# Block-wise causal attention and a gated feed-forward layer: four of six pairs of hidden chunks as seven block products in tiles 3 to 6, all six in tiles 7 and 8, all issued from written lists

## The chip, the cores and the metric

The kernel runs on one NeuronCore of a Trainium2 chip. The metric is the device time of one execution in microseconds (us), the median of the runs shown. A core has five engines with an instruction queue each, and each queue is worked off in order: PE (TensorE, the matrix engine; its weight loads are listed as PEld), DVE (VectorE), ACT (ScalarE), POOL (GpSimd) and SP (SyncE, here only a queue for transfers). Engines wait for each other by semaphores. The matrix engine writes to PSUM, eight banks of 128 x 512 float32; everything else is in SBUF, 128 partitions wide.

## The reference

```python
scores = scale * np.matmul(q, k.transpose(0, 1, 3, 2))      # q, k, v: 8 x 8 x 576 x 64
mask = block_i >= block_j                                   # blocks of 64 rows
attn = np.exp(...) / (np.sum(...) + 1e-09)
x = (attn @ v).transpose(0, 2, 1, 3).reshape(4608, 512)
gate = np.maximum(x @ w_gate, 0.0)                          # 512 x 1536
val = x @ w_val
return (gate * val @ w_out).astype(np.float32)              # 1536 x 512
```

## The kernel before, in words

**Tiles.** The 576 rows of a batch are cut into 512 and a tail of 64. Tile j (0 to 7) is the feed-forward layer of the 512 rows of batch j, tile 8 that of the eight tails together, 512 rows again. `x` lies transposed in `xT` (tile 8: `xTt`), four row groups of d_model by 512 tokens. The 1536 hidden columns are twelve chunks of 128. The work of tile j is interleaved on PE with the attention of batch j+1, which needs no more than that: per batch four rounds (one pair of heads each) of scores (`visit`, L465), exponentials on ACT (L470 and L477), products with v (L600, L614), their normalisation on DVE (L537 to L546) and a transpose by a transfer on SP's queue (L647). Loads of batch j+2 are 17 transfers issued by POOL (`load_qkv`, L353).

**A plain chunk.** Gate and value of chunk f are four matmuls each (`product`, L948; 128 x 512 elements out), ACT makes the ReLU into SBUF (`relu`, L958), DVE multiplies it with the value bank into `hT` (`hidden`, L968; L995 in tiles 7 and 8).

**Seven block products.** A product of two matrices cut 2 x 2 takes eight products of blocks, or, by Strassen's scheme, seven products of sums of blocks (numbered 1 to 7 in the code) and additions. The kernel uses this at two places. The projection to the output in tiles 2 to 8 (`seven_products`, L830) takes 84 matmuls of 256 columns per tile, numbered M below; DVE makes the sums of `hT` for it (`Sums`, L789), POOL and DVE made those of `wo` once (L706 to L720). And in tiles 7 and 8 the gate and value of a pair of chunks (`by_pairs`, `pair` and `times`, L1014; `PAIRS = (2, 4, 6)`: chunks 2 and 3, 4 and 5, 6 and 7) take 28 matmuls of 256 columns in place of 16 of 512. Here one matrix has the halves of d_model as rows and gate and value as columns, the other the halves of d_model and of the tokens. A pair uses three banks, `y`, `z` and `m1`. ACT copies y and z out, POOL adds these two copies (L1045), DVE subtracts them from m1 (L1048), adds the result to y and to z after further products were accumulated there (L1055, L1057), and two products give `hT` (L1058, on DVE or POOL; L1062). The sums of token halves, `x_sums`, are five DVE instructions per tile (L940), those of weights, `up_sum`, fifteen in tiles 5 and 6 (L747).

**What sets the order.** Each engine's queue is in the order in which the program emits. A generator `ffn_gen` emits the feed-forward work matmul by matmul; a table `AT` (and `STEADY` for later batches) says after how many of these each piece of attention, load or weight sum is emitted. Buffers are rotating: `psum_ffn` has three banks (`ffnp`), `psum_sc` two pairs of banks (`sc`), `psum_one` one (`one`), `ob` five SBUF buffers, `gate_sb` three, `stage` ten, `hT` three. An instruction that takes a buffer waits until the last reader of the buffer's former content has ended.

Of the kernel before, what the change touches and what calls it, by code (L numbers as in the profile page):

```python
# [17 lines left out]
def kernel(  # L18
# [22 lines left out]
    PAIRS = (2, 4, 6)  # L41
    BASE = {0: 0, 1: 512, 3: 896, 2: 1024}
    AW = 1600
    TW = 256

# [78 lines left out]
    class Early:  # L124
# [152 lines left out]
        def pe_mains(self, hp, evac, two=None, ts=(0, 1)):  # L277
            if two is None:
                two = {t: psum_ffn.tile([128, 512], BF, name="ffnp") for t in ts}
# [20 lines left out]
        def pe_tails(self, evac):  # L300

            tq = psum_ffn.tile([128, 4, 64], BF, name="ffnp")
            tk = psum_ffn.tile([128, 4, 128], BF, name="ffnp")
# [13 lines left out]
    def load_qkv(b, which, behind=None):  # L317
        for t in which:
            src = (q, k, v)[t]
            for c in range(NCH):  # L320
# [31 lines left out]
                for dst, part_of in pieces:  # L352
                    ins = nc.gpsimd.dma_start(dst, part_of)  # L353
                    after(ins, behind)
                    behind = None

    bfs = {}

    def dma_transposes(b):
        m, tl = bfs[b, 0], bfs[b, 1]  # L360
        for t in range(2):
# [4 lines left out]
        tails_by_dma(b, tl)  # L366
# [32 lines left out]
    def bank(where, dtype=FP):  # L399

        n = 512 if dtype == FP else 1024
        if where == "sc":
            return psum_sc.tile([128, 2, n], dtype, name="sc")[:, 0, :]
        if where == "one":
            return psum_one.tile([128, n], dtype, name="one")
        return psum_ffn.tile([128, n], dtype, name="ffnp")

    def scores(b, hp, pieces):
        sc = psum_sc.tile([128, 2, 512], FP, name="sc")
# [26 lines left out]
    def thirds():  # L436
        return (
            psum_one.tile([128, 512], FP, name="one"),
            psum_ffn.tile([128, 512], FP, name="ffnp"),
        )  # L440

    def visit(r):
# [3 lines left out]
        first = psum_sc.tile([128, 2, 512], FP, name="sc")  # L446
        second = psum_sc.tile([128, 2, 512], FP, name="sc")
# [26 lines left out]
        def exp_third():  # L474
            for hh in range(2):
# [4 lines left out]

        return exp_third, exp(first, 0), exp(second, 512)

    def last_keys(b):
# [10 lines left out]
        nc.scalar.activation(attnL[b % 2][:, 0:256], last, AF.Exp, scale=scale)  # L494

    def tail_visit(b):

        main = [psum_sc.tile([128, 2, 512], FP, name="sc") for _ in range(2)]
# [34 lines left out]
    def normalise(out, av, x=None):  # L533
        n = av.shape[1]
        rows = av.shape[0]
        recip = sb.tile([128, NCH], FP, name="recip", bufs=4)[0:rows, 0:n]
# [16 lines left out]
    def tail_av(b, g, x):  # L553

        av = psum_ffn.tile([128, 4, 65], FP, name="ffnp")
# [16 lines left out]
        recip = sb.tile([128, NCH], FP, name="recip", bufs=4)  # L572
# [18 lines left out]
    def products_with_v(r, hh, av):  # L591
# [17 lines left out]
        if b >= FIRST:  # L609
# [3 lines left out]
            for c in range(NCH):  # L613
# [9 lines left out]
                )  # L623
        normalise(xnats[r][:, :, 64 * hh : 64 * hh + 64], av, x)

    def head_av(r, hh, where):
        n = 5 if r // 4 >= FIRST else 4
        av = bank(where)[:, 0 : 65 * n].rearrange("q (p e) -> q p e", e=65)
        products_with_v(r, hh, av)
# [25 lines left out]
    store, late = [], []  # L655
# [65 lines left out]

    ups = {}

    def up_sum(n, which):
# [4 lines left out]
        if not ups:  # L729
            ups["free"] = [  # L730
                t[:, 512 * i : 512 * i + 512].rearrange("p (c f) -> p c f", c=2)
                for two in (new_bf(), new_bf())
                for t in two
                for i in range(4)
            ]
# [10 lines left out]
        t = ups[n, which] = ups["free"].pop(0)  # L746
        nc.vector.tensor_tensor(out=t, in0=a, in1=b, op=op)  # L747

    class Sums:
# [3 lines left out]
        def __init__(self, quads):  # L753
            self.quads = quads
            self.two = []
# [52 lines left out]
    def seven_products(j, quads, sums):  # L808
# [33 lines left out]
        early, last = ((0, 1, 2, 3), (4, 5)) if j < B - 1 else ((0, 1, 2, 4), (3, 5))  # L842

        def whole(to, which, new=True, cs=range(6)):
            for p in range(2):
                for c in cs:
                    times(half(to, p), which, p, c, new and (p, c) == (0, 0))
                    if c % 2:
                        yield

        def store_later(hi, n0, ob, p0=0, p1=2):
            if store:
                store.pop()()
            if j < B:
                store.append(lambda: put_block(j, hi, n0, ob, p0, p1))
            else:
                put_block(j, hi, n0, ob, p0, p1)

        y = psum_ffn.tile([128, 512], FP, name="ffnp")
        z = psum_one.tile([128, 512], FP, name="one")  # L860
        for to, which in ((y, 5), (z, 2)):
            yield from whole(to, which, cs=early)
        for to, which in ((y, 5), (z, 2)):
            yield from whole(to, which, new=False, cs=last)
        for q in range(3) if j >= B - 1 else ():
            sums.make_part(q, 1, 0, 2)
        g = sb.tile([128, 512], FP, name="ob", bufs=5)
        nc.scalar.copy(g, y)
        nc.vector.tensor_tensor(out=g, in0=z, in1=g, op=AX.add)
        for q in range(3) if j >= B - 1 else ():  # L870
            sums.make_part(q, 2, 0, 2)
        m1 = psum_ffn.tile([128, 512], FP, name="ffnp")
        yield from whole(m1, 1)
        nc.vector.tensor_tensor(out=g, in0=m1, in1=g, op=AX.subtract)
        if j == B - 1:
            x_sums(B, (1, 3))
        yield from whole(y, 3, new=False)
        c12 = sb.tile([128, 512], FP, name="ob", bufs=5)
        nc.scalar.copy(c12, y)  # L879
        store_later(0, 256, c12)  # L880
        c22 = sb.tile([128, 512], FP, name="ob", bufs=5)
        nc.gpsimd.tensor_tensor(out=c22, in0=g, in1=c12, op=AX.add)  # L882
        yield from whole(z, 4, new=False)
        c21 = sb.tile([128, 512], FP, name="ob", bufs=5)
# [930 lines left out]
```

## Time and profile before

| | |
|---|---|
| median of 3 runs | 351.77 us (351.35 to 353.55) |
| span of the profiled execution, first to last instruction | 350.5 us |
| what lies around the span, against the median | 1.27 us |
| tiles 0 and 1 with all that precedes them | 0 to 104.0 us |
| tile 2 | 104.0 to 141.08 us |
| tiles 3, 4 and 5, each | 37.15 us |
| tile 6 | 252.52 to 288.47 us, 35.95 us |
| tile 7 | 288.47 to 317.18 us, 28.71 us |
| tile 8 and the last stores | 317.18 to 350.5 us; last matmul about 345.7 us |
| granted TensorE clock | 0.999 of full |

The page gives no time of this execution but its span; the difference to the median is what is carried along for start and end. The tiles' borders are where a tile's plain matmuls (L948) begin in the chain that ended last. A matmul that the trace lists with 379 ns is not 379 ns of the engine: consecutive matmuls overlap, and what one costs is the distance from one start to the next.

### The profile page before, as it was taken

Reading aid. Unit: us, or ns where it says so; the run is one execution under the profiler, and the core shown is the slowest. Engines: PE = TensorE matmul, PEld = TensorE weight load, DVE = VectorE, ACT = ScalarE, POOL = GpSimd, SP = SyncE. Lnnn points to the kernel's source line nnn. Section 1 sums busy time; section 2 is a strip of 40 time slices with the busy share of each in tenths; the row PEclk is TensorE's granted clock in tenths of the full one; section 3 lists DMA queues with packets and bytes.
Section 4 is the critical chain, followed back from the end, with each engine's and each line's share of the span. In section 5 each row is a group of like instructions: output and inputs, shape, how many; then the busy total and the mean of one; then the engine's idle time right before and its main releaser. Section 6 shows DMA issues by size and latency. Waiting matters only on the chain.

```text
span 350.5 us, 8275 instructions
## 1 busy us (share of the span) xinstructions
PE 339.8 (97%) x3210; PEld 208.2 (59%) x3254; DVE 225.5 (64%) x564; ACT 185.2 (53%) x297; POOL 153.8 (44%) x194
## 2 busy tenths in 40 slices
PE   8999999999999999999999999999999999999994
PEld 3544455545445568545855576556755687687673
DVE  4853455667529784467547772668567867986892
ACT  5933766687235862666355545555366525423521
POOL 2767556576598902590149203950300022213213
PEclk9999999999999999999999999999999999999999
DMA  8999989999999994999459974999510031003005
GB/s 240 295 353 373 352 224 248 222 148 155 184 185 153 144 182 98 138 147 169 62 134 141 104 135 123 127 131 150 121 47 17 16 94 50 2 2 121 1 2 120
DMA packets 155399, 50.02 MB, mean 143 GB/s; under 512 B 134464, under 2 KB 151744, under 8 KB 155360
## 3 DMA queue, kind: packets, MB, share of 16 engines
q0 software_dynamic: 70528, 8.98, 49.1%
q1 hardware_dynamic: 77520, 32.52, 44.0%
q10 hardware_dynamic: 7312, 8.00, 7.8%
q8 instruction: 25, 0.41, 0.5%
q14 instruction: 14, 0.11, 0.1%
HBM read 37.75 MB, written 9.44 MB: 135 GB/s over the span
## 4 chain that ended last, share of the span: by engine, by line
PE 77%; DMA 14%; POOL 3%; issue 2%; DVE 2%; ACT 1%; SPq 1%; POOLq 0%; ACTq 0%
PE ffnp L948 39%; PE ffnp L830 12%; PE one L830 5%; PE sc L1014 3%; DMA stage<-in_moe_w_out_dram 3%; PE sc L465 3%; DMA xT<-xnat 2%; DMA stage<-in_moe_w_val_dram 2%; PE one L465 2%; DMA stage<-in_v_dram 2%; DMA stage<-in_moe_w_gate_dram 2%; PE ffnp L600 2%; PE one L600 2%; PE ffnp L1181 2%; PE one L1014 2%
## 5 line engine op out<-in xcount | busy, mean ns | idle before, releaser
L958 ACT ACTIVATE gate_sb<-ffnp 128x512 bf16<-128x512 f32 x95 | 57.1, 605 | 74.8 <-PE ffnp L948 66.5
L948 PE MATMUL ffnp<-xT,wg 128*128 128x512 bf16 x338 | 93.0, 379 | 1.7 <-issue 0.6
L948 PE MATMUL ffnp<-xT,wv 128*128 128x512 bf16 x309 | 87.7, 380 | 1.0 <-DVE hT L968 0.3
L968 DVE TENSOR_TENSOR hT<-gate_sb,ffnp 128x512 bf16<-128x512 bf16 x76 | 51.9, 683 | 46.0 <-PE ffnp L948 27.0
L948 PEld LDWEIGHTS <-wv 128*128 128x128 bf16 x384 | 35.4, 98 | 38.2 <-issue 4.6
L470 ACT ACTIVATE attnT<-sc 128x1024 bf16<-128x1024 f32 x56 | 57.0, 1042 | 0.0
L948 PEld LDWEIGHTS <-wg 128*128 128x128 bf16 x384 | 35.7, 98 | 35.0 <-issue 1.7
L882 POOL TENSOR_TENSOR ob<-ob 128x512 f32<-128x512 f32 x7 | 9.6, 1370 | 101.7 <-ACT ob L879 53.3
L830 PEld LDWEIGHTS <-stage 128*128 128x128 bf16 x420 | 40.3, 98 | 6.0
L789 DVE TENSOR_TENSOR stage<-hT 128x512 bf16<-128x512 bf16 (+2 forms) x82 | 37.8, 493 | 0.9
L600 PEld LDWEIGHTS <-attnT 128*128 128x128 bf16 x640 | 26.7, 98 | 11.9 <-DVE attnT L1241 0.9
L830 PE MATMUL ffnp<-stage 128*128 128x256 bf16 x252 | 31.4, 273 | 0.0
L353 POOL DMA_DIRECT2D v_bf<-in_v_dram x30 | 24.1, 869 | 6.1 <-DVE recip L537 2.6
L477 ACT ACTIVATE attnT<-one 128x512 bf16<-128x512 f32 (+1 forms) x28 | 15.0, 536 | 21.1 <-PE ffnp L465 21.1
L353 POOL DMA_DIRECT2D q_bf<-in_q_dram x20 | 17.9, 907 | 16.7 <-DVE hT L968 9.7
L1181 PE MATMUL ffnp<-wo,hT 128*128 128x512 bf16 x91 | 23.2, 379 | 0.3
L465 PEld LDWEIGHTS <-kTm 64*128 64x128 bf16 x384 | 11.0, 94 | 15.1 <-issue 7.9
L1045 POOL TENSOR_TENSOR ob<-ob 128x512 f32<-128x512 f32 x6 | 7.6, 1266 | 23.2 <-ACT ob L1044 23.2
L353 POOL DMA_DIRECT2D k_bf<-in_k_dram x20 | 17.8, 927 | 0.0
L830 PEld LDWEIGHTS <-hT 128*128 128x128 bf16 x168 | 16.4, 98 | 1.9
L465 PE MATMUL sc<-qTm,kTm 64*128 64x512 bf16 (+1 forms) x168 | 16.8, 305 | 0.0
L879 ACT COPY ob<-ffnp 128x512 f32<-128x512 f32 x7 | 4.1, 585 | 22.1 <-PE ffnp L830 22.1
(194 smaller groups left out, 556.0 us busy)
## 6 DMA issues: line engine op xcount, KB each, us to landing
out_dram<-ob ACTq DMA_DIRECT2D x28, 256.0 KB, 2.3
stage<-in_moe_w_val_dram SPq DMA_DIRECT2D x6, 512.0 KB, 8.7
stage<-in_moe_w_gate_dram SPq DMA_DIRECT2D x6, 512.0 KB, 8.2
stage<-in_moe_w_out_dram SPq DMA_DIRECT2D x6, 512.0 KB, 10.5
q_bf<-in_q_dram POOLq DMA_DIRECT2D x20, 128.0 KB, 4.2
k_bf<-in_k_dram POOLq DMA_DIRECT2D x20, 128.0 KB, 5.2
v_bf<-in_v_dram POOLq DMA_DIRECT2D x20, 128.0 KB, 7.0
stage<-in_v_dram SPq DMA_DIRECT2D x19, 128.0 KB, 5.5
```

The lines of the kernel that those rows point to most:

```text
L353: ins = nc.gpsimd.dma_start(dst, part_of)
L465: nc.tensor.matmul(o, kTm[b % 2][head_of(hh), c, hp, :], qT, start=True, stop=True)
L470: return lambda: nc.scalar.activation(at[:, :, lo : lo + 512], sc, AF.Exp, scale=scale)
L477: nc.scalar.activation(at[:, hh, 1024 : 1024 + w], third[hh][:, 0:w], AF.Exp, scale=scale)
L600: nc.tensor.matmul(av[:, p, :], at[:, col : col + 128], v_bf[b % 2][:, c, h, :], start=(p == 0), stop=(c == p), skip_group_check=True,)
L789: nc.vector.tensor_tensor(out=out.rearrange("p (c n) -> p c n", c=m), in0=a, in1=b, op=op)
L830: nc.tensor.matmul(to, sums.of(c)[which][:, 128 * p : 128 * p + 128], right, start=first, stop=(c == 5), skip_group_check=True,)
L948: nc.tensor.matmul(to, (wg, wv)[t][f // 4][:, c, 128 * (f % 4) : 128 * (f % 4) + 128], x[:, c], start=(c == 0), stop=(c == 3),)
L958: nc.scalar.activation(gate_sb, gate, AF.Relu)
L968: nc.vector.tensor_tensor(out=h, in0=gate_sb, in1=val, op=AX.mult)
L1014: nc.tensor.matmul(to[:, 256 * k : 256 * k + 256], left[:, c, 128 * k : 128 * k + 128], right[:, c], start=new and (k, c) == (0, 0), stop= ...
L1181: nc.tensor.matmul(op, hT[f][:, 128 * s : 128 * (s + 1)], wo[f // 4][:, f % 4, n0:n1], start=(f == 0), stop=(f == 11),)
```

## The change

Up to tile 2 every engine issues the same instructions in the same order, and PE does so up to the end of tile 2's plain chunks. From there on:

- `PAIRS` names all six pairs. In tiles 3 to 6 the pairs 1, 2, 3 and 5 (chunks 2 to 7, 10 and 11) are made by seven products and chunks 0, 1, 8 and 9 plainly; in tiles 7 and 8 all six pairs by seven products. These are 4 x 4 + 2 x 3 = 22 pairs more.
- The weight sums (`up_sum`, tokens U) become twenty in tile 2 on DVE, placed by `U_AT`, and ten in tile 6 (`ONLY`), seven of them on POOL. Sums 6 and 7 overwrite the weights that they are made of; the others lie in `stage`, `sevens` and `attnT` buffers.
- Tiles 3 to 8 are not emitted by `ffn_gen` any more but by `program(j)`, which reads a list of tokens. `p13` is half of product 3 of pair 1 (four matmuls), `p1m` the subtraction of pair 1, `p1H` and `p1L` its two products for `hT`; `M3` is two matmuls of the output's product 3; `g0 v0 r0 h0` a plain chunk; `s1012` a sum of `hT`; `oa` to `o7` the output's vector work and `S0` to `S3` its stores; `A`, `E`, `C`, `V`, `N`, `T` the pieces of an attention round; `l`, `w`, `d` loads and transposes of the next batch but one. Tiles 3 to 6 share one list.
- `ON_POOL` names which additions and products run on POOL: four H and three s per tile and the output's `od` in tiles 3 to 6, eleven in tile 7, twelve and `od` in tile 8.
- The output's products run in the order 3, 4, 1, 5, 2, 6, 7 in tile 2, and as listed later; before it was 5, 2, 1, 3, 4, 6, 7.
- Rotating buffers in PSUM, `ob` and `gate_sb` become named ones, whose turn is written in `SLOTS`; `PAIR_BANK` names the banks of each pair.

```diff
-    PAIRS = (2, 4, 6)
+    PAIRS = (0, 2, 4, 6, 8, 10)
+    OUT_2 = (3, "oa", 4, "ob", 1, "om", 5, "oy", 2, "oz", "S0", "oc", "od", 6, "o6", "S1", 7, "o7", "S2")
+    ORDER_3_6 = """
+        l0 A0 E0u X1 X3 X4 X6 X7 g0 E0s E0t g0*3 v0*4 p12 r0 h0 C01 p15*2 g1*2 K l1 g1
+        p12 g1 l2 l3 l4 E0f C00 k p1a p1b p1s V00 N00 p13*2 l5 l6 l7 V01 U41 N01 U02 p1r
...
+        p55 p5b s1101 p5a w3 p5s v8*3 h8 p51 p54 V10 p51 d0 N10 d1 T1 p53 E2f p53 p5r
+        p54 g9*4 p5l r9 p56*2 p57 v9 p57 M3 p5m s1012 p5y p5z v9*2 p5H s1212 p5L v9 h9
+        M3 s2012 s1001 C20 A3 E3t U47 M3*2 E3s T0 d2 M4 M3 w4 w5 M4 M3 M4*2 s2001 s2112
...
+        s2201 M6 M7 M6*4 om oc o6 od M7*3 U05 U07 M7*2 U46 S2 o7
+    """
+    ORDER_7 = """
+        p12 p02 p12 p1b p05*2 p0a X1 X3 X4 X6 X7 p15 p02 p0b p15 p11*2 p1a p1s p03*2 p14
+        p01 p13*2 Y1 p1m p04 p01 p0s p0m p0r p06 p04 p1r p16*2 p1y p1H p06 p25 p0y p25
...
+    PAIR_BANK = {
+        (3, 1): ('sc', 'ffn', 'sc'),
...
+    U_AT = {'U15': 300, 'U12': 306, 'U11': 312, 'U16': 386, 'U17': 389, 'U25': 320, ...}
...
     def up_sum(n, which):
-        t = ups[n, which] = ups["free"].pop(0)
-        nc.vector.tensor_tensor(out=t, in0=a, in1=b, op=op)
+        if which in (6, 7):
+            t = a
+        else:
...
+        on(f"U{n}{which}").tensor_tensor(out=t, in0=a, in1=b, op=op)
...
+    def program(j):
...
+        def pair(n, what):
+            y, z = st.get((n, "y")), st.get((n, "z"))
+            name = f"{j}{n}{what}"
+            if what == "a":
+                st[n, "a"] = ob()
+                nc.scalar.copy(st[n, "a"], y)
...
+            elif what == "s":
+                a = st[n, "a"]
+                on(name).tensor_tensor(out=a, in0=a, in1=st.get((n, "b"), z), op=AX.add)
+            elif what == "m":
+                a = st[n, "a"]
+                nc.vector.tensor_tensor(out=a, in0=st[n, "m"], in1=a, op=AX.subtract)
...
+                if what == "H":
+                    on(name).tensor_tensor(out=h[:, :, 256:512], in0=split(st[n, "high"]), in1=split(st[n, "b"]), op=AX.mult)
...
+                    nc.vector.scalar_tensor_tensor(out=h[:, :, 0:256], in0=split(st[n, "a"]), scalar=0.0, in1=split(st[n, "low"]), op0=AX.max, op1=AX.mult)
...
         ffn(10**6)
+        for j in range(3, B + 1):
+            do, end = program(j)
+            for item in ORDER[j].split():
+                t, _, times = item.partition("*")
+                if j not in ONLY.get(t, (j,)) or (t[0] in "lwd" and j == B - 2):
+                    continue
+                for _ in range(int(times or 1)):
+                    do(t)
+            end()
```

More of the change, by code (lines that the diff above doesn't have):

```diff
@@ L720, in weight_differences, with on @@
             eng.tensor_tensor(out=d, in0=d, in1=n, op=AX.subtract)
+    def on(name):
+        return nc.gpsimd if name in ON_POOL else nc.vector
     ups = {}
     def up_sum(n, which):
[L729 to L735, printed above, removed]
         i, lo = divmod(PAIRS[n], 4)
@@ L859, in seven_products @@
[L859 to L881, printed above, removed]
@@ L909 @@
+        return products, do
     xsum = {}
```

685 lines of the change are left out of this document (464 added, 221 removed).

## The prediction
> **What bounds the kernel now.** I read three views in this order: the busy times of the page, the table of stretches cut at the tile borders, and the chain that ended last.
>
> ```profile
> PE 339.8 (97%) x3210; PEld 208.2 (59%) x3254; DVE 225.5 (64%) x564; ACT 185.2 (53%) x297; POOL 153.8 (44%) x194
> ```
>
> PE is busy for 339.8 of 350.5 us. Whether that is an average over different limits is told by the stretches (columns: stretch, length, busy us and instructions of PE, PEld, DVE, ACT, POOL, then clock, transfers, GB/s):
>
> ```profile
> 178.22:215.37 37.15, 36.78 (x364) 22.76 (x370) 22.74 (x60) 20.17 (x33) 16.30 (x19) 1.00 1.48 127
> 288.47:317.18 28.71, 28.55 (x215) 21.14 (x216) 23.11 (x42) 11.57 (x21) 7.79 (x6) 1.00 0.11 37
> 317.18:350.50 33.32, 28.70 (x216) 20.94 (x214) 22.33 (x39) 11.58 (x21) 8.15 (x7) 0.98 0.18 48
> ```
>
> From 141 us to the last matmul at 345.7 us PE idles about 0.4 us per tile. DVE has 14 us to spare in a tile 3 to 6 but only 5.6 in tile 7. The chain gives the price of a matmul (start, length, line, count):
>
> ```profile
> 211.56 2.62 PE ffnp L830 x24
> 291.51 0.87 PE sc L1014 x8
> 292.38 0.86 PE ffnp L948 x4
> ```
>
> A 512-column matmul costs 0.2163 us (0.865 for four), a 256-column one 0.1091 (2.62 for 24), so halves cost 0.9% more than wholes.
>
> **What PE gains.** A plain pair is 16 x 0.2163 = 3.46 us, a pair by seven products 28 x 0.1091 = 3.05; 0.406 less. 22 pairs more: **8.9 us**. The tiles' needs become 35.5 us (3, 4, 5), 34.3 (6) and 27.5 (7, 8). With PE as full as now the span is 350.5 - 8.9 = 341.6 us.
>
> **What the others get.** Two DVE instructions in a row start 0.60 apart (104.60 and 105.20 us, each listed with 0.69), so I count 0.62 for 128 x 512 out of PSUM or float32. The sums of `hT` go by 0.34 (512) and 0.22 (256), x sums 0.41, a normalised head 0.70, a corner 0.15. Per tile 3 to 5:
>
> - DVE: 5 x sums 2.1, 4 plain products 2.5, m, y, z of four pairs 7.4, one s 0.6, four L 2.5, 18 sums 5.4, 8 heads 5.6, 8 corners 1.2, five for the output 3.1: 30.4 us of 35.5. Before it was 22.7 of 37.15.
> - ACT: 11.5 for exponentials and about 23 copies and ReLUs at 0.49 (distance between such rows in a row), 25 us.
> - POOL: 17 loads, 14.0 (rows of 0.66 to 0.89), four H at 1.17 (row L1058 on POOL), three s and `od` at 1.27 (row L1045): 23.8 us.
>
> Tile 7: DVE 7 x sums 2.9, one s 0.6, 18 of m, y, z 11.2, 6 L 3.7, sums 5.4, six for the output 3.7: 27.5 us against 27.5 of PE. Its POOL: 6 H and 5 s, 13.4. Tile 8: DVE 24.2, POOL 15.9. No engine is over PE by its sum, but DVE is level with it in tile 7, and starts that tile about 1.1 us late: `o7` follows tile 6's last matmul.
>
> **What the sums leave out.** Two rows show it.
>
> ```profile
> 291.01 1.27 POOL L1045 TENSOR_TENSOR ob<-ob 128x512 f32<-128x512 f32 x1 [3.07 <-ACT ob L1044]
> 291.79 1.11 DVE L940 TENSOR_TENSOR perm<-xT 128x512 bf16<-128x512 bf16 x2
> 248.04 0.41 DVE L747 TENSOR_TENSOR k_bf<-wv 128x512 bf16<-128x512 bf16 x1
> 248.19 1.72 POOL L882 TENSOR_TENSOR ob<-ob 128x512 f32<-128x512 f32 x1 [14.92 <-ACT ob L879]
> ```
>
> Two x sums take 1.11 us where two in a row take 0.75 (313.85). One of them is the 780 ns one of its group, against a median of 418: it began at 291.79, POOL's addition ended at 292.28, and it ran after that. At 248.19 it is the other way: POOL's addition takes 1.72 instead of 1.27 beside a DVE sum. DVE instructions that read PSUM (L995 at 291.18) kept their 0.69 beside POOL. So an instruction of DVE with two inputs in SBUF and one of POOL hold each other up. The Trainium skill states it as a rule (SBUF — State Buffer, section "SBUF: two separate sides"): whichever of the two starts first has the shared ports for its whole length and the other is blocked; the rows agree, and the rule speaks against this change.
>
> Of DVE's work, instructions with two SBUF inputs (x sums, sums of `hT`, L, `oc`, `od`, s) are 10.6 us in a tile 3 to 5, 13.8 in tile 7 and 10.5 in tile 8. With POOL's arithmetic (9.8, 13.4, 15.9) that makes 20.4 us of 35.5, 27.2 of 27.5 and 26.4 of 27.5 which exclude each other. Before, in tiles 7 and 8, POOL's 15.9 us of arithmetic cost DVE 0.94 us (two x sums of 780 and 858 against 418), 6%, at a quarter of PE's time; its share now doubles, so I take 12%. The bounds are 0 and 100%.
>
> **Where it reaches PE.**
>
> *Tiles 3 to 6.* The tightest place is `p57 M3 ... p5z v9*2 p5H s1212 p5L v9 h9 M3 s2012 s1001 C20 A3 E3t M3*2`. Let p57 end at 0. The third M3 multiplies with what p5L writes. PE gets to it at 0.22 + 0.65 (v9) + 0.22 + 0.88 (A3, by subtracting the known matmuls from 37.15) = 1.97. DVE can start 0.29 after the last matmul's slot (195.22 to 195.51): p5z at 0.29, s1212 at 0.91, p5L from 1.25 to 1.94, and PE goes on 0.05 after (107.93 to 107.98). That just fits. But p5H runs on POOL as soon as y is added, from 0.38 to 1.55, and s1212 and p5L have two SBUF inputs each: s1212 at 1.55, p5L from 1.89 to 2.58, PE at 2.63: 0.65 us late, **2.6 us** in four tiles. Elsewhere DVE has no listed work for 2 us before p57, which takes up other delays. From below the cost is 0 (the order of H and s1212 may fall out otherwise), from above each of eight POOL instructions delays PE by half its length, 5 us per tile.
>
> *Tile 2* gets twenty sums of weights. DVE was already without a pause from 104.6 to 111.3, and PE had waited:
>
> ```profile
> 107.98 1.02 PE L948 MATMUL ffnp<-xT,wv 128*128 128x512 bf16 x4 [0.27 <-DVE hT L968]
> ```
>
> U15 falls into DVE's 3.0 us pause before 104.60, U12 (0.34) ahead of the product that PE waits for; from 112 on DVE pauses for 4 us in all, about what the next ten cost. **0.4 us**; 0 if PE's banks give more, 6.8 if all twenty pass through. The eight of the output part come before the last normalised heads and delay the transpose of `xT` for tile 3 by 2 us; it landed 3 us before its use.
>
> *Tiles 7 and 8.* DVE needs 27.5 + 24.2, starts 1.1 late and loses 12% of POOL's 29.3, 3.5: 56.3 against PE's 55.0, **1.3 us**. Bounds: 0 at 4% and less, 27 at 100%.
>
> *Moved transfers.* POOL's 17 loads now stand among its H and s. The last for k (l10) is issued some 18.6 us into the tile, after 18.2 us of POOL's list; such loads land 5.2 us later (median), and the transposes made of them are first read in the next tile: 11 us of cover. On SP, T3 follows the last normalised head; it lands 3.9 us later (median of 24), and PE reads it after 17 x 0.218 of M, A0 and three of g0, 5.2 us. The cover is 1.3 us, where it was about 3; a slower landing (9.2 at most) would come out one for one. I count nothing for both.
>
> *The end* stays: 4.8 us from the last matmul (345.7) through a half subtraction to the store. The new order of the output's products in tile 8 needs no sums at first; before it waited for none on PE either, so nothing.
>
> **The sum.** 350.5 - 8.9 + 2.6 + 0.4 + 1.3 = 345.9 us of span. The median lies 1.27 above the profiled span; nothing before tile 2 changes, so I carry it: **347.2 us**, 1.3% less. A measurement of this kernel tells about 1% from no change.
>
> **The rivals.**
>
> *Everything is hidden.* Banks and the lists leave room, and the blocks fall where DVE waits anyway. For it: 0.4 us of idle PE per tile today, and only four blocked instructions in the trace. Against it: DVE's 5 us of slack per tile instead of 14, none in tile 7. 341.6 + 1.3 = 342.9 us.
>
> *The gain is eaten.* DVE and POOL exclude each other for more than the 12%. With a share p of POOL's arithmetic lost to DVE, tiles 7 and 8 cost 29.3p - 2.2, the rest stays at 3.0. At 28% the whole 8.9 is gone: 351.8 us. For it speaks that 27.2 of 27.5 us exclude each other in tile 7; against it that POOL's instructions start after a wait for DVE or ACT, mostly when DVE goes on with PSUM.
>
> *Slower.* The same mechanism, in the same place, from 40% on. DVE then reaches PE's banks: `y`, `z` and `m` of a pair are free only after p_y, p_z and p_m, all on DVE, and with two pairs in flight all usable banks are held. At one half: 341.6 + 3.0 + 12.4 + 1.3 = 358.3 us. Tiles 3 to 6 join in only beyond 52%, where 30.4 + 9.8p passes 35.5.
>
> That the change does nothing can be left out: 22 pairs have 22,528 columns fewer.
>
> **Chances.** Forecast (344 to 349.5) 0.55, all hidden 0.17, gain eaten (349.5 to 355.3) 0.15, slower 0.13. By these, faster by over 1% (below 348.3) is 0.17 + 0.46 = 0.63, within 1% 0.24, slower 0.13. The range 342.7 to 352.5 takes in the lower bound and half of the eaten gain; it leaves out the slower case and little else.
>
> **What would show it.** In the profile after: tiles 3 to 5 at 36.1 to 36.3 us each (35.5 if hidden); a PE wait of about 0.65 us for the product L1415 once per tile, before the third M3; x sums, sums of `hT` and L1415 well over their medians of 0.42 and 0.69, up to 1.5, wherever POOL's H or s runs; tile 7 and 8 together 56 to 57 us from first to last matmul. I am wrong if tiles 3 to 6 take over 37 us, if PE waits elsewhere (for transfers, for ACT), or if tile 7's DVE is not near 95% busy.

## The result and the profile after

The changed kernel takes **369.42 us** (median of 4 runs, 367.39 to 371.05) where the kernel before takes 351.67 (351.35 to 353.55): 1.0495 times as long, 95% interval 1.0454 to 1.0536. Predicted were 347.2 us, with a range up to 352.5; the sign is wrong. The profiled execution is the shortest of the four, with a time of 367.39 us and a span of 365.6. The longest has a span of 369.3 and a mean granted clock of 0.985 instead of 0.993; one thing that can make them differ shows in a later run, below.

First the busy times of the page and the shares of the chain that ended last, after:

```profile
PE 339.3 (93%) x3485; PEld 234.7 (64%) x3518; DVE 288.8 (79%) x682; ACT 207.6 (57%) x341; POOL 209.0 (57%) x237
PE 69%; DVE 20%; issue 7%; ACT 2%; POOL 1%; DVEq 0%; POOLq 0%
```

PE's busy time is what it was (339.8 before), so its share of the span fell from 97 to 93%. In the chain DVE now has 20%; before it had 2%. The stretches say where (columns: stretch, length, busy us and instructions of PE, PEld, DVE, ACT, POOL, clock, transfers, GB/s), here tiles 4, 6, 7 and 8, cut at the last matmul of each output:

```profile
176.84:214.15 37.31, 36.04 (x415) 27.54 (x416) 32.37 (x81) 24.02 (x40) 23.65 (x26) 1.00 1.30 126
...
251.42:291.58 40.16, 36.53 (x416) 27.70 (x417) 36.38 (x84) 24.41 (x40) 17.43 (x15) 1.00 0.16 42
291.58:327.11 35.53, 30.52 (x255) 25.05 (x252) 34.33 (x57) 14.89 (x27) 16.16 (x13) 0.95 0.07 23
327.11:365.60 38.49, 28.77 (x254) 24.34 (x251) 31.01 (x53) 14.91 (x27) 18.53 (x14) 0.97 0.17 50
```

In tile 7 DVE is busy for 34.33 of 35.53 us, in tile 6 for 36.38 of 40.16. Cut in the same way, the tiles compare thus (us):

| | tile 3 | 4 | 5 | 6 | 7 | 8 | end |
|---|---|---|---|---|---|---|---|
| before | 37.14 | 37.15 | 37.15 | 37.15 | 28.70 | 28.70 | 4.79 |
| after | 37.76 | 37.32 | 37.26 | 40.16 | 35.53 | 33.30 | 5.19 |
| DVE's excess, after | 1.74 | 1.73 | 1.75 | 5.40 | 7.41 | 5.17 | |

Tile 2 ended at 139.72 before and at 139.08 after. The differences add up to the 15.1 us between the spans: 14.4 of it are in tiles 6 to 8. The last row is worked out from the trace: by how much DVE's instructions lasted longer than the median of their form, summed over a tile. Before, this is 0.04 to 0.07 in a tile 3 to 6 and 0.4 and 0.5 in tiles 7 and 8. Where it comes from shows in the rows of DVE's sums of `hT` and of its products for `hT` (count, then min/median/max in ns), first in the kernel before, then in the changed one:

```profile
L789 DVE TENSOR_TENSOR stage<-hT x82: 284/422/693, 110.2 to 341.4; 128x512 bf16<-128x512 bf16 x44, 128x1024 bf16<-128x1024 bf16 x28, 128x256 bf16<-128x256 bf16 x10
L1062 DVE SCALAR_TENSOR_TENSOR hT<-ob x6: 684/685/685, 295.8 to 335.8; 128x512 bf16<-128x512 f32 x6
```

```profile
L992 DVE TENSOR_TENSOR stage<-hT x120: 276/411/1502, 110.1 to 357.6; 128x512 bf16<-128x512 bf16 x78, 128x256 bf16<-128x256 bf16 x38, 128x1024 bf16<-128x1024 bf16 x4
L1415 DVE SCALAR_TENSOR_TENSOR hT<-ob,q_bf x12: 676/682/1760, 301.0 to 352.6; 128x512 bf16<-128x512 f32 x12
```

In the changed kernel the longest sum takes over three times the median, the longest product 2.6 times; before, no sum takes over 0.70 us, which is the length of the widest ones, and no product over 0.69. Three places in tile 4 account for 1.6 of its 1.7 us. From the timelines of POOL, DVE and PE in the changed kernel (start, length, engine, line):

```profile
194.11 1.15 POOL L1401 TENSOR_TENSOR hT<-gate_sb,ob 128x512 bf16<-128x512 bf16 x1 [0.24 <-DVE ob L1393]
...
196.91 1.56 POOL L1377 TENSOR_TENSOR ob<-ob,ob 128x512 f32<-128x512 f32 x1
201.59 1.16 POOL L1401 TENSOR_TENSOR hT<-gate_sb,ob 128x512 bf16<-128x512 bf16 x1 [3.12 <-DVE ob L1393]
```

```profile
194.62 1.19 DVE L1415 SCALAR_TENSOR_TENSOR hT<-ob,ob 128x512 bf16<-128x512 f32 x1
...
197.61 1.01 DVE L992 TENSOR_TENSOR stage<-hT 128x256 bf16<-128x256 bf16 x1
198.54 0.67 DVE L1445 TENSOR_TENSOR hT<-gate_sb,ffnp 128x512 bf16<-128x512 bf16 x1
...
202.25 0.78 DVE L992 TENSOR_TENSOR stage<-hT 128x512 bf16<-128x512 bf16 x1
```

```profile
199.27 1.02 PE L1322 MATMUL ffnp<-xT,wg 128*128 128x512 bf16 x4 [0.76 <-DVE hT L1445]
...
203.70 0.50 PE L1033 MATMUL ffnp<-wo,hT 128*128 128x256 bf16 x3 [0.25 <-DVE hT L1415]
```

Each of the three DVE instructions (p2L, s1101, s1212 of the list) starts while a POOL product or addition runs, and ends 0.15 to 0.55 us after it. The second is the costly one: s1101 lasts 1.01 instead of 0.29, behind it on DVE stands the product h8, which reads a bank that PE's g9 needs, and PE waits 0.76 us. The third reaches PE as the wait of L1033 that was predicted (0.25 listed, 0.44 by the distance of the starts). The first has no wait of its own; it delays what stands behind it in DVE's queue, which pauses for under 0.2 us up to s1101.

In tile 7 nearly every POOL instruction has such a partner. From the timelines of POOL, DVE and PE, and the stretches of PE around the worst place (length, PE busy, clock):

```profile
299.71 2.29 POOL L1401 TENSOR_TENSOR hT<-gate_sb,k_bf 128x512 bf16<-128x512 bf16 x2 [4.17 <-DVE k_bf L1393]
301.96 3.13 POOL L1377 TENSOR_TENSOR ob<-ob,k_bf 128x512 f32<-128x512 f32 x2
```

```profile
301.03 1.52 DVE L1415 SCALAR_TENSOR_TENSOR hT<-ob,q_bf 128x512 bf16<-128x512 f32 x1
302.47 0.68 DVE L1396 TENSOR_TENSOR ob<-ffnp,ob 128x512 f32<-128x512 f32 x1
303.07 2.30 DVE L992 TENSOR_TENSOR stage<-hT 128x512 bf16<-128x512 bf16 x2
```

```profile
306.00:308.00 2.00, 0.60 (x4) 1.00 0.00 0
...
310.00:312.00 2.00, 2.00 (x11) 0.50 0.00 0
312.00:314.00 2.00, 2.00 (x18) 0.89 0.04 8
```

One product and two sums, 0.68 and 0.75 us when undisturbed, take 3.8 us together, and POOL's two additions take 3.13 where two take 2.5. PE is then starved, and from 309.0 to 312.4 its granted clock is 0.50, so that each pair of 256-column matmuls takes 0.43 us instead of 0.22: another 1.7 us in tile 7, as an estimate from these distances.

### The profile page after: what moved, and what is told of

Same layout as the page of the kernel before. It is cut to its first block, busy times and chain, and to the rows that moved or that the text cites. A ratio compares the mean times of both kernels' runs of the same rounds, so it can differ in the third digit from the quotient of the medians.

```text
span 365.6 us, 9070 instructions
## 1 busy us (share of the span) xinstructions
PE 339.3 (93%) x3485; PEld 234.7 (64%) x3518; DVE 288.8 (79%) x682; ACT 207.6 (57%) x341; POOL 209.0 (57%) x237
## 4 chain that ended last, share of the span: by engine, by line
PE 69%; DVE 20%; issue 7%; ACT 2%; POOL 1%; DVEq 0%; POOLq 0%
PE ffnp L1162 15%; PE ffnp L1033 10%; PE sc L1348 6%; PE ffnp L1265 6%; PE ffnp L1348 5%; PE ffnp L1322 5%; PE one L1033 4%; DVE stage L992 4%; PE one L1348 2%; DVE hT L1415 2%; DVE ob L1382 2%; PE sc L611 2%; DVE ob L1396 2%; DVE ob L1393 2%; ACT attnT L575 2%
## 5 line engine op out<-in xcount | busy, mean ns | idle before, releaser
L992 DVE TENSOR_TENSOR stage<-hT 128x512 bf16<-128x512 bf16 (+2 forms) x120 | 53.5, 478 | 0.3
L1033 PEld LDWEIGHTS <-stage 128*128 128x128 bf16 x420 | 40.4, 98 | 5.9 <-issue 1.4
L1080 POOL TENSOR_TENSOR ob<-ob,ob 128x512 f32<-128x512 f32 x7 | 8.9, 1266 | 52.1 <-issue 37.9
L1162 PE MATMUL ffnp<-xT,wg 128*128 128x512 bf16 x130 | 36.2, 379 | 0.6
L1172 ACT ACTIVATE gate_sb<-ffnp 128x512 bf16<-128x512 f32 x35 | 20.5, 599 | 27.4 <-PE ffnp L1162 22.9
L1348 PEld LDWEIGHTS <-stage 128*128 128x128 bf16 x288 | 28.0, 99 | 12.1 <-issue 3.5
L1033 PE MATMUL ffnp<-stage 128*128 128x256 bf16 x252 | 32.1, 273 | 1.0 <-DVE ob L1396 0.8
L1162 PE MATMUL ffnp<-xT,wv 128*128 128x512 bf16 x108 | 31.3, 380 | 0.2
L1182 DVE TENSOR_TENSOR hT<-gate_sb,ffnp 128x512 bf16<-128x512 bf16 x28 | 19.1, 684 | 13.8 <-PE ffnp L1162 11.2
L1401 POOL TENSOR_TENSOR hT<-gate_sb,ob 128x512 bf16<-128x512 bf16 x16 | 18.9, 1178 | 13.6 <-DVE ob L1393 13.4
L623 ACT ACTIVATE attnT<-one 128x512 bf16<-128x512 f32 (+1 forms) x28 | 15.1, 538 | 16.1 <-PE ffnp L611 8.4
L1377 POOL TENSOR_TENSOR ob<-ob,k_bf 128x512 f32<-128x512 f32 x11 | 16.7, 1524 | 12.8 <-ACT k_bf L1374 12.4
L1377 POOL TENSOR_TENSOR ob<-ob,ob 128x512 f32<-128x512 f32 x12 | 16.7, 1388 | 11.9 <-ACT ob L1374 7.3
L1401 POOL TENSOR_TENSOR hT<-gate_sb,k_bf 128x512 bf16<-128x512 bf16 x12 | 14.6, 1223 | 15.3 <-DVE k_bf L1393 15.3
L1322 PE MATMUL ffnp<-xT,wg 128*128 128x512 bf16 x64 | 19.5, 379 | 3.1 <-DVE hT L1445 3.1
```

What stands on the lines that cost most here:

```text
L992: nc.vector.tensor_tensor(out=out.rearrange("p (c n) -> p c n", c=m), in0=a, in1=b, op=op)
L1033: nc.tensor.matmul(to, sums.of(c)[which][:, 128 * p : 128 * p + 128], right, start=first, stop=(c == 5), skip_group_check=True,)
L1162: nc.tensor.matmul(to, (wg, wv)[t][f // 4][:, c, 128 * (f % 4) : 128 * (f % 4) + 128], x[:, c], start=(c == 0), stop=(c == 3),)
L1172: nc.scalar.activation(gate_sb, gate, AF.Relu)
L1322: nc.tensor.matmul(to, (wg, wv)[t][f // 4][:, c, 128 * (f % 4) : 128 * (f % 4) + 128], x[:, c], start=(c == 0), stop=(c == 3),)
L1348: nc.tensor.matmul(st[key][:, 256 * k : 256 * k + 256], left[:, c, 128 * k : 128 * k + 128], right[:, c], start=new and (k, c) == (0, 0), ...
```

## The experiments

**Theory**: DVE is held up by POOL's arithmetic wherever both read SBUF (the shared ports of the prediction), and what DVE loses, PE loses. **Rivals**: DVE's sheer load is too high, whatever POOL does; POOL's results come late; or the written lists and named buffers cost the time.

### POOL writes only

All of POOL's H and s and its weight sums are two memsets each of the same place, at the same point in its queue; these results are left out.

```diff
-                on(name).tensor_tensor(
-                    out=a, in0=a, in1=st.get((n, "b"), z), op=AX.add
-                )
+                for _ in range(2):
+                    after(nc.gpsimd.memset(st[n, "a"], 0.0), st["ins", n, "b"])
...
+                    for _ in range(2):
+                        after(nc.gpsimd.memset(h[:, :, 256:512], 0.0), st["ins", n, "y"])
```

> Left out: what POOL computes in H, s and its weight sums in tiles 3 to 8; each is replaced by two memsets of the same output (0.52 us each by the row of such a memset), which read nothing and wait for the same copy or addition. Theory of the shared ports: DVE's instructions with two SBUF inputs go back to their medians (0.41 for a sum of 512, 0.69 for L), tiles 3 to 5 take 35.5 to 36.0 us, tile 6 about 35, tiles 7 and 8 together 56 to 59 us instead of 68.7, the span 344 to 349 us. Rival, DVE's load and the written order (DVE busy for 31 to 36 us per tile whatever POOL does): tiles 3 to 5 stay over 36.8, the span over 358.

Measured: 351.44 us in one run. Tiles 3 to 8 were as the theory has them, 36.37, 36.02, 35.95, 35.95, 28.18 and 28.21 us, but tile 2, which the edit does not touch, ended at 143.80. So it was run again.

> The same kernel as e1 once more (POOL's H, s and weight sums are two memsets each, their results left out), timed in rounds. In e1 tiles 3 to 8 were near PE's floors, but tile 2, which the edit does not touch, ended 4.7 us late behind one transpose by transfer. If that was a single event, the time is 345 to 347 us, 1.3 to 2% below the kernel before; if it belongs to the kernel, 351 us again. The theory of the shared ports says nothing on tile 2 and expects tiles 3 to 8 at 36.0 to 36.4 (four times) and 28.2 (twice) in both cases.

Measured: **346.75 us**, the median of five, 0.9858 of before (0.9843 to 0.9873). The profiled execution is the longest of the five, 348.37 us; its tile 2 ended at 140.71, the other tiles took the same to 0.01 us. DVE's excess is 0.15 in a tile 3 to 5, 0.5 in tile 6 and under 0.1 in tiles 7 and 8. From the row of DVE's sums of `hT` and the stretches (tiles 5, 7 and 8 of this second run):

```profile
L996 DVE TENSOR_TENSOR stage<-hT x120: 280/409/693, 111.7 to 338.6; 128x512 bf16<-128x512 bf16 x78, 128x256 bf16<-128x256 bf16 x38, 128x1024 bf16<-128x1024 bf16 x4
```

```profile
213.11:249.06 35.95, 35.93 (x418) 27.57 (x416) 30.79 (x81) 24.02 (x40) 22.11 (x33) 1.00 1.40 132
285.00:313.18 28.18, 28.11 (x254) 24.38 (x252) 26.93 (x57) 14.80 (x27) 12.62 (x25) 1.00 0.09 28
313.18:341.40 28.22, 28.12 (x254) 24.36 (x251) 25.31 (x52) 14.87 (x27) 13.83 (x26) 1.00 0.12 36
```

DVE issues the same 81 instructions in tile 5 and 57 in tile 7, in 1.6 and 7.4 us less, and PE is full. The lists and the named buffers are thereby cleared, and so is the load that DVE has in these lists: with 26.93 of 28.18 us it does not hold PE up in tile 7. The Trainium skill (SBUF — State Buffer, section "SBUF: two separate sides") restricts the lock between DVE's instructions with two SBUF inputs and POOL to POOL instructions that read SBUF; the 102 memsets in place of H and s, 0.53 us each, agree.

### POOL reads one input

As before, but with two copies in place of the two memsets; POOL's results are again left out.

```diff
-                    after(nc.gpsimd.memset(st[n, "a"], 0.0), st["ins", n, "b"])
+                    after(nc.gpsimd.tensor_copy(st[n, "a"], st[n, "b"]), st["ins", n, "b"])
```

> As the kernel whose POOL only writes, but each H, s and weight sum of POOL is two copies with one SBUF input (about 0.6 us each). If any reading by POOL blocks DVE, as the Trainium skill states it (SBUF — State Buffer, section SBUF: two separate sides), the span is within 4 us of the changed kernel's 365.6; if it takes two inputs on POOL's side, it is that of the kernel whose POOL only writes. Rival, DVE's load: both the same, over 358.

Measured: 358.88 us; tiles 37.21, 36.76, 36.37, 38.58, 32.10, 31.51. Neither forecast held: the span of 357.1 us lies 8.5 below that of the changed kernel and well above that of the kernel whose POOL only writes. A POOL instruction with one input holds DVE up too, but for less: DVE's excess is 1.2, 1.2, 0.8, 3.7, 3.8 and 2.8 us, half to two thirds of that of the changed kernel; of the time lost there against POOL writing only, it loses a third to two thirds. That two short copies (0.6 to 0.8 us each) let DVE in between, where one addition of 1.27 us does not, would explain it; no run shows it by itself.

### All of it on DVE

```diff
-        2oc 2od 31H 31s 32H 33H 33s 35H 35s 3od 41H 41s 42H 43H 43s 45H 45s 4od
...
+    ON_POOL = {"2oc", "2od", "3od", "4od", "5od", "6od", "8od"}
```

> All H, s and weight sums on DVE, POOL keeps od. Shared ports: no blocked DVE instruction except beside od, but seven, eleven and twelve instructions of 0.62 us more on DVE: 32.5 - 1.7 + 4.3 = 35.1 us of DVE in tiles 3 to 5 (37 to 38 us each), about 33.7 and 33 in tiles 7 and 8, so 362 to 368 us, no worse than the changed kernel by more than 3. Rival, load: every added instruction lengthens the tile, 3 x 4.3 + 8 + 6.8 + 7.4 us more, over 380.

Measured: 380.31 us; tiles 40.34, 39.90, 39.82, 41.45, 36.88, 34.53. POOL's arithmetic, and with it every block but that of `od`, is gone, and the kernel is slower still: tile 5 carries seven more DVE instructions (7 x 0.62 = 4.3 us) and takes 3.9 us more than with POOL writing only. The 362 to 368 us expected from the ports are missed by 12, and the figure of the rival, over 380, is what came. The ports are not the whole of it, then. In these lists DVE has no time to give, whether it is blocked or works.

### The three meeting places taken apart

In tiles 3 to 6 s1101 goes behind N10, p2L ahead of N11, and p5H to DVE.

```diff
-        U01 p3H V11 N11 p3l l10 A2 E2t p2L E2u p37*2 p3z s1201 p3L E2s p52*2 p55 C21 v8
-        p55 p5b s1101 p5a w3 p5s v8*3 h8 p51 p54 V10 p51 d0 N10 d1 T1 p53 E2f p53 p5r
+        U01 p3H V11 p3l l10 A2 E2t p2L N11 E2u p37*2 p3z s1201 p3L E2s p52*2 p55 C21 v8
+        p55 p5b p5a w3 p5s v8*3 h8 p51 p54 V10 p51 d0 N10 s1101 d1 T1 p53 E2f p53 p5r
```

> Only the list of tiles 3 to 6: s1101 stands behind N10 instead of beside p5s, p2L ahead of N11 and so ahead of p3H, and p5H runs on DVE. Shared ports: the three blocked DVE instructions per tile (0.50, 0.72 and 0.36 us) go, tiles 3 to 5 take 36.0 to 36.6 us instead of 37.3, tile 6 1 us less; 365.6 - 4 = 361 to 363 us of span. Rival, load: DVE has 0.6 us more in each tile, 366 to 368.

Measured: 367.05 us, 1.0446 of before (1.0373 to 1.0519). Tiles 3 to 5 took 37.14, 36.70 and 36.62, 0.63 less each; DVE's excess there fell from 1.74 to 0.12. Of these 1.6 us, 0.62 went back to p5H on DVE. The tiles come out just above the 36.0 to 36.6 expected. The time of the whole decides nothing between the two readings: its runs spread over 4.7 us and overlap those of the changed kernel. Tile 8, which the edit does not touch, took 34.93 us instead of 33.30. DVE was busy there for as long as in the changed kernel (30.58 and 30.40 us), but PE's clock was halved once more, at about 350 us, and PE was busy for 30.24 instead of 28.61. So such a stretch, which one execution has and another has not, is worth 1.6 us of the difference between executions of the same tiles.

### A dose of DVE time without any block

POOL writes only, and DVE gets seven memsets per tile 3 to 6, at the three places where it was blocked.

```diff
-        U01 p3H V11 N11 p3l l10 A2 E2t p2L E2u p37*2 p3z s1201 p3L E2s p52*2 p55 C21 v8
-        p55 p5b s1101 p5a w3 p5s v8*3 h8 p51 p54 V10 p51 d0 N10 d1 T1 p53 E2f p53 p5r
-        p54 g9*4 p5l r9 p56*2 p57 v9 p57 M3 p5m s1012 p5y p5z v9*2 p5H s1212 p5L v9 h9
+        U01 p3H V11 N11 p3l l10 A2 E2t Z*2 p2L E2u p37*2 p3z s1201 p3L E2s p52*2 p55 C21 v8
+        p55 p5b Z*3 s1101 p5a w3 p5s v8*3 h8 p51 p54 V10 p51 d0 N10 d1 T1 p53 E2f p53 p5r
+        p54 g9*4 p5l r9 p56*2 p57 v9 p57 M3 p5m s1012 p5y p5z v9*2 p5H Z*2 s1212 p5L v9 h9
...
+            elif k == "Z":
+                nc.vector.memset(zeros, 0.0)
```

> As e5 (POOL only writes, its H, s and weight sums left out), but in tiles 3 to 6 DVE gets seven memsets of 0.22 to 0.27 us per tile: three ahead of s1101, two ahead of p2L, two ahead of s1212, where the changed kernel's DVE was blocked for 0.72, 0.50 and 0.36 us. That is 1.5 to 1.9 us of DVE time at the same places with no blocking at all. Theory, only DVE's lost time matters and the lists leave it no slack there: tiles 3 to 6 go from 36.0 to 37.2 to 37.8 us, what the changed kernel's tiles 3 to 5 took. Rival, DVE has room and it was POOL's results coming late that cost the time: 36.0 to 36.4 us.

Measured: 354.33 us; tiles 3 to 6 at 38.26, 37.91, 37.84 and 37.84, tiles 7 and 8 unchanged at 28.17 and 28.21. The group of the memsets and the stretch of tile 5:

```profile
L1510 DVE MEMSET zeros<- 128x256 uint32 x28 | 7.6, 272 | 2.3
```

```profile
215.35:253.19 37.84, 36.21 (x418) 27.58 (x416) 32.42 (x88) 24.02 (x40) 22.13 (x33) 1.00 1.33 130
```

Seven memsets of 0.272 us are 1.90 us; tile 5 became 1.89 us longer. At these three places DVE's time comes out one for one, although DVE is idle for over 5 us of the tile. The rival, that DVE has room and POOL's results come late (36.0 to 36.4 us), is out: POOL does here what it did in the run without DVE's memsets.

### Tiles 7 and 8 undone

Tiles 7 and 8 get lists with the three pairs of before, and tile 6 loses its ten weight sums. (Other than the expectation says, chunks 10 and 11 of tiles 7 and 8 are here computed with weights that sums 6 and 7 of pair 5 had overwritten; the work is the same. This holds for the next run too.)

```diff
     ORDER_7 = """
-        p12 p02 p12 p1b p05*2 p0a X1 X3 X4 X6 X7 p15 p02 p0b p15 p11*2 p1a p1s p03*2 p14
+        g0*4 r0 P X1 X3 X4
+        p15*2 p1a p12*2 p1b p1s v0*4 h0 X6 X7 p11*2 p1m p13*2 p1r p14*2 p1l g1*4 r1 p16*2 p1y p17*2 p1z p1H p1L v1*4 h1
...
```

> Tiles 3 to 6 as changed, but tiles 7 and 8 with the three pairs of before (chunks 2 to 7) in the order of before, written as lists, and so tile 6 without its ten weight sums. Whole computation. Shared ports: tiles 3 to 5 stay at 37.3 to 37.8 us, tile 6 falls from 40.2 to 37.3, tiles 7 and 8 come back to 28.7 to 28.9: 139.1 + 149.7 + 57.6 + 4.8 = 351.2 us of span, 352 to 353 us, no measurable difference to before. If the loss of tiles 6 to 8 lay in the named buffers or the written lists as such, tiles 7 and 8 stay over 30 us and the time over 355.

Measured: 355.88 us, 1.0149 (1.0105 to 1.0192). Tiles 37.76, 37.31, 37.24, 37.25, 29.62, 29.64. This is over the 352 to 353 us expected and just over the 355 named for the rival, that the lists or the named buffers cost the time; but tiles 7 and 8 stay under the 30 us named with it, and the end alone took 6.0 us instead of 4.8. Tile 6 without the sums is a tile like 4 and 5, so the ten sums cost it 2.9 us. Tiles 7 and 8 recover 9.6 of 11.4 us. Of the missing 0.9 in each, the next run's trace lists 0.47 as a wait of PE, ahead of the output's first product, for DVE's product of a plain chunk; it comes from the list.

With the list of tiles 3 to 6 mended as in the fourth run, and s1212 and p5H moved behind p5L:

```diff
-        p54 g9*4 p5l r9 p56*2 p57 v9 p57 M3 p5m s1012 p5y p5z v9*2 p5H s1212 p5L v9 h9
-        M3 s2012 s1001 C20 A3 E3t U47 M3*2 E3s T0 d2 M4 M3 w4 w5 M4 M3 M4*2 s2001 s2112
+        p54 g9*4 p5l r9 p56*2 p57 v9 p57 M3 p5m s1012 p5y p5z v9*2 p5L v9 p5H h9
+        M3 s2012 s1001 C20 s1212 A3 E3t M3*2 E3s T0 d2 M4 M3 w4 w5 M4 M3 M4*2 s2001 s2112
```

> As e7, and in tiles 3 to 6 the list mended where POOL and DVE met: s1101 behind N10, p2L ahead of N11, p5H on DVE behind p5L, s1212 behind C20. Whole computation. Shared ports: e4 had no blocked pair over 0.4 us left and one PE wait of 0.66 us for p5L, which p5H and s1212 no longer delay. So tiles 3 to 6 at 36.0 to 36.3, tiles 7 and 8 at 28.7 to 28.9: 139.3 + 144.6 + 57.6 + 4.8 = 346.3 us of span, 347 to 348 us, about 1.2% below before. If DVE's load alone bounds tiles 3 to 6, whatever POOL does, moving p5H to DVE makes them 36.6 or more, and the time is 349.5 or more.

Measured: 353.44 us, 1.0054 (1.0042 to 1.0066). Tiles 3 to 6 took 37.12, 36.70, 36.63, 36.63, as in the fourth run. Moving p5H behind p5L changed nothing, so the expected 36.0 to 36.3 us is missed and the reading by load (36.6 or more) holds.

### Corners and p5H

The corner memsets of tiles 3 to 6 go to POOL; tiles 7 and 8 get four pairs by a list of my own. Then p5H goes back to POOL as well, and in a third run p5H alone. Of the one long line of `ON_POOL` only the names that are added are shown.

```diff
     ON_POOL = set("""
...
+        0C 1C 2C 3C
...
+        35H 45H 55H 65H
```

> Whole computation. Tiles 3 to 6 as in e8, but the eight corner memsets per tile (64x128, 0.165 us each, tokens C) run on POOL, which e5 and e6 showed not to hold DVE up when it only writes. Tiles 7 and 8 with four pairs (chunks 2 to 7, 10 and 11) by a list of my own. Theory: in tiles 3 to 6 each us of DVE comes out one for one above 36.0 us (e6), p5H costs 0.62, eight corners give 1.3 to 1.5 back, so tiles 3 to 6 are bound by PE: 35.5 to 35.8 us. Tiles 7 and 8: 28.2 to 28.9. 139.3 + 142.6 + 57 + 4.9 = 343.8 us of span, 345 us, 1.9% below before. Rival: POOL, busy with loads in the first half, makes the corners late, and PE waits for them before the products with v: tiles 3 to 6 at 36.6 or more.

> As e9, with p5H of tiles 3 to 6 back on POOL (1.17 us there). It takes 0.62 us from DVE and blocks what DVE does with two SBUF inputs beside it, p5L and s2012, by up to 0.6 us. With DVE relieved by the corners both come out at PE's bound: within 0.3 us per tile of e9, 344 to 346 us. If DVE still bounds the tiles, the difference to e9 shows whether 0.62 us of load or the block costs more.

> As e10, with the corners back on DVE. Load theory: e8's tiles 3 to 6 of 36.63 less 0.62 plus what p5H blocks (0.3 to 0.6): 36.3 to 36.6. Tiles 7 and 8 as in e9. Span 348 to 349 us.

Measured: 365.62 us (1.0408, 1.0382 to 1.0435), 365.19 (1.0401, 1.0380 to 1.0422), and 361.46 in one run. My list for tiles 7 and 8 was poor (32.6 to 32.8 us each in all three), so only tiles 3 to 6 tell: 38.59, 39.99, 38.37, 36.23 with the corners; 40.26, 38.45, 40.07, 36.31 with both; 36.79, 36.34, 36.27, 36.27 with p5H alone. The rival for the corners holds. What PE waits for in tiles 3 to 6 of the first of the three (us in total, times, longest):

```profile
PE ffnp L722 <- POOL attnT L1492: 6.6, 3, 2.2
```

In POOL's queue the corners stand behind loads, once per tile 3 to 5 for 2.2 us. (The tile of 39.99 us has a mean clock of 0.96 besides.) Tile 6, which has no loads, shows what the corners are worth: 0.40 us with p5H on DVE (36.63 in the run before, 36.23 here), nothing with p5H on POOL (36.27 and 36.31). p5H on POOL is worth 0.36 us per tile by itself (36.63 to 36.27): its 0.62 us of work against a block of 0.24. So either brings the tile to 36.3, and the second adds nothing; there PE is busy for 36.25 of 36.27 us, and the 35.5 to 35.8 us expected were not reached.

### Four pairs in tiles 7 and 8, and none more than before

The same tiles 3 to 6, and another list for the four pairs of tiles 7 and 8:

```diff
-        p25*2 p2a p22*2 p2b p2s g8*4 r8 p21*2 p2m p23*2 p2r p24*2 p2l s0002 v8*4 h8 p26*2 p2y p27*2 p2z p2H p2L s0102
+        p25*2 p2a p22*2 p2b p2s g8*4 r8 p21*2 s0002 s0102 p2m p23*2 p2r p24*2 p2l v8*4 h8 p26*2 p2y p27*2 p2z p2H p2L
...
-        p36*2 p3y p37*2 p3z g9*4 r9 p3H p3L p56*2 p5y p57*2 p5z p5H p5L v9*4 h9 M3*2 M4*2 s1102 M1*2 M3*4 oa s2101 s2112 M4*4 ob
+        p36*2 p3y p37*2 p3z p3H p56*2 p5y p57*2 p5z g9*4 r9 p3L p5L v9*4 h9 p5H M3*2 M4*2 M1 M3*4 oa s1102 s2101 s2112 M4*4
```

> Whole computation. Tiles 3 to 6 as in e11 (list mended, H and s on POOL, corners on DVE, no weight sums in tile 6), tiles 7 and 8 with four pairs and another list, in which DVE's sums of hT lie where e11's DVE waited and the last plain chunk stands between the last pair and the output's products. In e11 PE waited 4.4 us per tile 7 and 8, in all but 0.4 us for DVE. Theory of DVE's dense stretches and the shared ports: tiles 3 to 6 at 36.3 (36.8 the first), tiles 7 and 8 at 28.2 to 28.8, so 139.3 + 145.7 + 57 + 4.9 = 346.9 us of span, 348.2 us, 1% below before. Rival, POOL and DVE still meet in tiles 7 and 8 for 1 us or more in each: 349.5 to 351 us, no difference to before.

Measured: 352.42 us, 1.0024 (0.9989 to 1.0059). Tiles 3 to 6 came out at 36.79, 36.36, 36.27, 36.27, tiles 7 and 8 at 30.63 and 29.95. This is over the 348.2 us expected. DVE's excess in tiles 7 and 8 is 1.5 and 1.6 us, as the rival has it (1 us or more in each): its sums s0002 and s0102 took 2.11 us instead of about 1.0 beside p2s on POOL.

Last, tiles 7 and 8 with the three pairs of before and the weights of chunks 10 and 11 restored:

```diff
+            elif k == "R":
+                restore(int(of[0]), int(of[1]))
...
+        d, b = {6: (u[:, 0:2, f], g[:, 0:2, f]), 7: (g[:, 2:4, f], u[:, 2:4, f])}[which]
+        nc.vector.tensor_tensor(out=d, in0=d, in1=b, op=AX.add)
```

> Whole computation. Tiles 3 to 6 as in e11; tiles 7 and 8 with three pairs and the engines' shares of before (chunks 2 to 7), the list mended so that no sum of hT stands ahead of a product that PE waits for; the two sums that overwrote weights of chunks 10 and 11 are taken back by two DVE additions at the end of tile 6. If the pairs in tiles 3 to 6 pay for themselves once POOL and DVE are kept apart, tiles 3 to 6 stay at 36.3 (36.8 the first, up to 36.8 the last), tiles 7 and 8 come to 28.7 to 28.9, and the span to 139.3 + 146 + 57.5 + 4.9 = 347.7 us, 349 us, 0.7% below before. If part of their cost is handed on to tile 7 (stores, buffers, the output's last sums), tile 7 is over 29.5 and the time within 0.3% of before.

Measured: **350.10 us**, 0.9962 of before (0.9947 to 0.9976). The stretches of tiles 6, 7 and 8:

```profile
248.61:284.88 36.27, 36.25 (x418) 27.50 (x417) 31.66 (x83) 24.02 (x40) 10.12 (x9) 1.00 0.17 47
284.88:313.58 28.70, 28.70 (x218) 21.04 (x216) 24.98 (x45) 11.68 (x21) 6.41 (x6) 1.00 0.12 39
313.58:342.28 28.70, 28.70 (x218) 21.04 (x215) 22.06 (x38) 11.58 (x21) 6.31 (x6) 1.00 0.12 32
```

PE is full in all three. Nothing is handed on from tile 6; the pairs in tiles 3 to 6 pay once POOL and DVE are kept apart, and this version is faster than both kernels, by 0.4% over the one before. Tiles 3 to 6 are together 2.9 us shorter than before, of 6.5 that their 16 pairs save by the price of a matmul.

## Why the prediction was wrong

Tile 5 in seven runs puts the theory and the load in one table (DVE's busy time includes its blocked time):

| tile 5 | DVE busy | length |
|---|---|---|
| POOL writes only | 30.79 | 35.95 |
| p5H back on POOL, list mended | 31.14 | 36.27 |
| list mended, p5H on DVE | 31.48 | 36.62 |
| three places taken apart | 31.42 | 36.62 |
| changed kernel | 32.40 | 37.27 |
| dose of memsets | 32.42 | 37.84 |
| all on DVE | 34.95 | 39.82 |

The length follows DVE's time at 0.8 to 1.2 us per us, with the place making the difference, while DVE's share of the tile never exceeds 88%. Point by point:

- **What PE gains (8.9 us): too high.** With POOL only writing, tiles 3 to 8 together are 5.3 us shorter than before. The price of a matmul holds (0.11 us for 242 of 251 distances in tile 7 there), but tiles 3 to 5 come to 36.0, not 35.5, and tiles 7 and 8 to 28.2, not 27.5: a few short waits and switches per tile that I had taken as gone.
- **Tile 2 (+0.4): wrong sign, small.** It ended 0.64 us earlier.
- **Tiles 3 to 6 (2.6 us): a step that failed in kind.** The mechanism and the place were right: PE waits for L1415 before the third M3. But "elsewhere DVE has no listed work for 2 us before p57, which takes up other delays" is not so: from p2L to p5L DVE is occupied almost without a pause (2.90 of 3 us busy from 194.84, 2.96 from 197.84, 2.87 from 200.84), and a block at the front of this stretch, s1101 for 0.72, arrives at PE as 0.76. I had compared sums per tile, 30.4 of 35.5, and looked for slack in one place only. Tiles 3 to 5 lost 1.3 us each against POOL writing only, not 0.65. The slower rival's "tiles 3 to 6 join in only beyond 52%" fell with it: they joined in at 18% (1.74 of the 9.7 us that POOL's arithmetic takes undisturbed).
- **Tile 6: left out of the sum.** Ten weight sums, seven on POOL, were named but never priced. They cost 2.9 us, by the run without them.
- **Tiles 7 and 8 (1.3 us): the step that failed in size, and the largest.** The share of POOL's time lost to DVE was taken as 12%, by doubling the 6% of before. (The two x sums named for it are 0.80 us longer together than 418 ns each, not 0.94, which makes 5%.) It is 12.6 us of 29.3, 43%. Against POOL writing only, the two tiles lost 12.4 us, of which about 1.7 are the halved clock. The prediction's own sum of DVE's time, 52.8 us and the share of 29.3, gives 65.4 us for the two tiles with 43%; they took 68.8. So the path, DVE's queue, was right, and the share was mis-sized. That it rose by itself is a reading that no run isolates: a blocked DVE falls behind, and its sums, no longer in the gaps that the list has for them, queue up beside the next POOL instruction, which is blocked in turn. The figure was at hand in the text as "27.2 of 27.5 exclude each other"; from that the slower rival was the nearer case, and it was given 0.13. Even its 358.3 us at one half is 11 short, for the reasons above.
- **The clock** was not in any rival. The starved PE ran at half clock for 3.4 us in tile 7, 1.7 us.
- **Transfers, ACT and the end: right.** No transfer makes PE wait in tiles 3 to 8, and the end grew by 0.4 us.

Together these make up the 19.7 us between the span forecast (345.9) and the one measured (365.6): 3.6 in what PE gains, 5.6 in tiles 3 to 6 (8.2 lost against POOL writing only, tile 6's 4.2 among them, where 2.6 was counted), 11.1 in tiles 7 and 8, 0.4 in the end, less 1.0 in tile 2.

Of the signs that I had named for being wrong, two came true: tiles 3 to 6 over 37 us, and PE waiting elsewhere (for h8's bank in tiles 3 to 5; in tiles 7 and 8 for p_m, p_y, p_z, for a p_H on POOL and for x sums). The third did not: tile 7's DVE is 97% busy, about the 95% forecast, but with 7.4 us of it blocked.

Two of the single runs were late in tile 2, by 4.7 us (POOL writing only) and 4.5 (p5H alone), and there the same mechanism shows where no edit touched the kernel. POOL's sums of `wo` stood behind loads that waited for a transfer of `k_bf`, and ran on until 109.4 and 109.5 us, where they end at 103.2 in the changed kernel. DVE's five differences and sums of weights between two products of plain chunks, which read SBUF alone, took 4.0 us beside them instead of 1.2, and PE waited 2.8 us for the second of these products. What is left of the lateness is in part waits for transfers (1.5 us in the first of the two).

What stays open: how much of the changed kernel's spread (span 365.6 to 369.3) is the halved clock and how much is late sums of `wo`; and whether six pairs in tiles 7 and 8 could be listed without blocks, which was not tried.

## What to carry to other kernels

Before work goes to an engine with time to spare, sum the receiving engine and its neighbours over the stretches of a few us in which they are dense, not over the stage: 5 us of idle time per tile gave no slack at the place that mattered. Where two engines exclude each other, count the price by the time for which both want the same thing at the density after the change; doubling today's small share is no estimate (it gave 12%, the run 43%). And a queue of an engine that also issues loads is no place for short work that PE waits for.

## What the runs showed of the hardware

- A POOL instruction that only writes SBUF (memset, 0.53 us) does not hold DVE up; one that reads one input does. DVE's instructions of 128 x 512 with an input in PSUM kept their 0.67 to 0.69 us in the changed kernel throughout.
- The blocked instruction does its work after the other has ended, not slower beside it: the three of tile 4, of 0.68, 0.29 and 0.41 us, end 0.55, 0.15 and 0.28 us after POOL's, each time 0.13 less than their own length. A sum of `hT` of 0.41 us took up to 1.50 in this way, a product of 0.68 up to 1.76, and POOL's addition of 1.27 up to 1.72.
- After 3.3 us in which PE was busy for 1.0 (305.7 to 309.0), its granted clock was 0.50 for 3.4 us and then 1.00 again. The Trainium skill (TensorE: Matmul & The Clock Gate, section "What's actually happening") has a halved clock after an idle window of about 3.4 us and its return after a busy one. The lengths agree; but PE was not idle throughout in this trace, so a window that is mostly idle was enough here.
